# A linear-attention and GLU block on one core: VectorE work, transposes and a last tile moved between the steps

## The chip, the core and the metric

The kernel runs on one core of one Trainium2 chip. The metric is the device time of one execution in microseconds, the median of several runs. The profile beside it is that of one execution. Engines in it: PE is TensorE, PEld its weight loads, DVE VectorE, ACT ScalarE, POOL GpSimd, SP the engine that issues the transfers.

## The reference

One transformer block over 2048 tokens of width 512, all in float32. Six vectors of 512 (shift, scale and gate for each half) come from `silu(c) @ w_mod`.

```python
h = _layernorm(x) * (1 + ca) + sa
qkv = (h @ wqkv) ...                      # 32 heads of 16
pq, pk = phi(q), phi(k)                   # phi(t) = where(t > 0, t + 1, exp(t)) + 1e-6
kv = einsum("bhsd,bhse->bhde", pk, v);  z = einsum("bhsd->bhd", pk)
o = einsum(pq, kv) / (einsum(pq, z) + 1e-6)
x = x + ga * (o @ wo)
h = _layernorm(x) * (1 + cb) + sb
x = x + gb * (((h @ w_gate) * (h @ w_up)) @ w_down)     # F = 1376
```

## The kernel before

**Numbers and splits.** Every matrix that TensorE multiplies is held as a high part, rounded to fp32r on ScalarE, and a low part, the difference, taken on VectorE or GpSimd (`split`, lines 182 to 184). A product is then three matmuls: high by high, high by low, low by high.

**Tiling.** The 2048 tokens are four chunks (ch) of 512, each of four token tiles (j) of 128; token tile i is 4 ch + j. F is cut into ten tiles of 128 and one of 96. The three last ones, f0, f1 and f2 (`lone`, f2 has 96 rows), are worked plainly for chunks 0 and 1: `gate_up` makes the gate and the up product of one F tile (24 matmuls of 128x512, lines 683 to 702), multiplies them (line 699) and splits the result into kh and kl; `down` multiplies these with the down weights into four accumulator banks and its `take` adds them to x (`evac`, line 677). All else of the GLU goes through `block` (lines 855 to 903): for two chunks and one F tile at a time it forms seven products of half matrices instead of eight, in the order p1, p5, p6, p2, p7, p3, p4, six matmuls each, on four fixed PSUM banks a, b, c, d. ScalarE copies bank to bank (line 842), VectorE adds (lines 892 and 896) and multiplies (line 865). `down_group` (lines 905 to 919) is the down product of a group of F tiles; at the very end `by_tile` makes it finish one token tile after the other, and `evac` adds and sends each to the output (lines 677 and 679).

**The attention's second half.** For each token tile, `den_c` divides phi(q) by the denominator (line 509), `turn` transposes it (`turn_a`, line 578) and splits it (`turn_h` on ScalarE, line 582; `turn_l` on VectorE, line 586), `y_seed` writes the old x into a bank (line 605), `y_a` adds twelve matmuls of y to it (line 614), and `y_b` copies the result to x (line 619) and takes its statistics (lines 225, 226). When the four tiles of a chunk are there, `rstd_of` takes the power on GpSimd (line 234), `nmr_of` the product of mean and rstd on VectorE (line 237), `xhat` normalises on ScalarE (line 243), and `ln2_turn` transposes (line 250) and modulates (lines 262, 272, 273); chunks 2 and 3 go to DRAM (`kept`) and come back as the left operands of `block` (`Left`, whose sums are line 755). `Right` holds the right operands: `sums` (line 805), `high` (lines 816 and 819, ScalarE) and `lows` (line 823, GpSimd).

**What sets the order.** The schedule is manual: each engine issues its instructions in the order in which the code records them, and waits for the semaphores that its operands and buffers need. So the program text from line 1003 on is the order of each engine's queue. PSUM has two pools of four banks, `acc` and `bank`; a tile that is asked for while all are in use waits for the oldest to be read. `ffn` (lines 957 to 997) is a generator that yields after each product of `block`, and `fill(n)` (line 999) lets n of them be recorded; so the sequence of `fill` calls between lines 1128 and 1150 sets how the products of the first blocks stand among the last y products. Inside a block, `p6` scales the down weights (line 970), `p7` records the split of the next block's right operand, `p3` the split of the down weights (high on ScalarE, low on GpSimd), `p4` the sums of the block after it.

Of the kernel before, what the change touches and what calls it, by code (L numbers as in the profile page):

```python
# [11 lines left out]
ALU = mybir.AluOpType  # L12
AX = mybir.AxisListType

P = 128
# [7 lines left out]
def tile_adaln_block(  # L23
# [12 lines left out]
    nc = tc.nc  # L36
    ctx.enter_context(tc.manual_schedule())
    _, S, D = x.shape
    F = w_gate.shape[1]
    KD = D // P  # L40
    NJ = 4
# [10 lines left out]
    ov = out[0].rearrange("(c p j) d -> c j p d", p=P, j=NJ)  # L52
# [26 lines left out]
    def acc_bank():  # L79
        return T(ps_acc, "acc")  # L80
# [311 lines left out]
    rows, cols = {}, {}  # L392
# [27 lines left out]
    ahead = {2: proj(2, wk)}  # L420
    for i in range(NT):
        ch, j = divmod(i, NJ)
# [81 lines left out]
    def den_c(*tiles):  # L504

        for i in tiles:
            ch, j = divmod(i, NJ)
            p3 = phq[i].rearrange("p (h i) -> p h i", i=DH)
            nc.vector.scalar_tensor_tensor(p3, p3, EPS_PHI, dens[ch][:, j].unsqueeze(2).to_broadcast([P, NH, DH]),
                                           op0=ALU.add, op1=ALU.mult)  # L510
# [20 lines left out]
    ps = proj(6, wq)  # L531
    fs, tt = [], []
    for k in range(KD):
        f = B("n")
# [9 lines left out]
    for g in range(KD):  # L544
        a, b = g * P, (g + 1) * P
# [4 lines left out]
    ps = proj(8, wq)  # L550
# [9 lines left out]
    ps = proj(9, wq)  # L560
# [27 lines left out]
    def turn(i):  # L588
        turn_a(i)
        turn_h(i)  # L590
        turn_l(i)
# [7 lines left out]
    def y_seed(i, of=acc_bank):  # L599

        yps[i] = of()
        if of is bank:

            nc.tensor.matmul(yps[i], wp[0][0][:, :P], wp[0][0], start=True, stop=True)
        nc.scalar.activation(yps[i], xts[i // NJ][i % NJ], AF.Copy)
# [10 lines left out]
    def y_b(i):  # L616
        ch, j = divmod(i, NJ)
        ps = yps.pop(i)
        nc.scalar.activation(xts[ch][j], ps, AF.Copy)
        norm2[ch].stats(j, of=ps)  # L620

    def y_step(i, *more, late=(), q=None, turn=True, seed=acc_bank):

        if q is not None:
            ps = proj(q, wq)
        if turn and i + 1 < NT and i + 1 not in pqs:
            turn_a(i + 1)
        y_a(i)
        if i + 1 in tps:
            turn_h(i + 1)  # L630
            turn_l(i + 1)
        if i - 1 in yps:
            y_b(i - 1)
        if q is not None:
            q_a(q, ps)
        if seed and i + 1 < NT:
            y_seed(i + 1, seed)
        for do in more:
            do()
        for do in late:  # L640
            do()

    norm2 = {}
# [3 lines left out]
    wf = {}  # L647
# [23 lines left out]
    def prepare(f):  # L671
        return lambda: (scale_down(f), split_ffn(f))

    def evac(ch, dn, js=range(NJ), last=False):
        for j in js:
            xt = xts[ch][j]
            nc.vector.tensor_tensor(xt, dn[j], xt, op=ALU.add)  # L677
            if last:
                nc.sync.dma_start(ov[ch, j], xt)

    hs = {}

    def gate_up(ch, f):

        n = fts[f][1]
        gps, ups = bank(), bank()
        for w, ps in ((wf[f][0], gps), (wf[f][1], ups)):
            for k in range(KD):
                hh, hl = norm2[ch].t[k]
                nc.tensor.matmul(ps[:n], w[0][:, k], hh, start=k == 0, stop=False)  # L690
                nc.tensor.matmul(ps[:n], w[0][:, k], hl, start=False, stop=False)  # L691
                nc.tensor.matmul(ps[:n], w[1][:, k], hh, start=False, stop=k == KD - 1)  # L692

        def rest():
            g = B("phi")
            h = B("kh", dt=F32R)
            l = B("kl", dt=F32R)
            nc.scalar.activation(g[:n], gps[:n], AF.Copy)
            nc.vector.tensor_tensor(g[:n], ups[:n], g[:n], op=ALU.mult)
            split(g[:n], h[:n], l[:n])  # L700
            hs[ch, f] = h, l
        return rest

    def down(ch, js=range(NJ), ahead={}, parts=(lone,)):

        dn = {j: acc_bank() for j in js}
        for step, (part, j) in enumerate((part, j) for part in parts for j in js):
            for do in ahead.get(step, ()):
                do()
            a, b = j * P, (j + 1) * P  # L710
            for f in part:
                n = fts[f][1]
                (hh, hl), (dh, dl) = hs[ch, f], wf[f][2]
                nc.tensor.matmul(dn[j], hh[:n, a:b], dh[:n], start=f == lone[0], stop=False)
                nc.tensor.matmul(dn[j], hh[:n, a:b], dl[:n], start=False, stop=False)
                nc.tensor.matmul(dn[j], hl[:n, a:b], dh[:n], start=False, stop=f == lone[-1])
        return lambda: evac(ch, dn, js)
# [184 lines left out]
        also("p4")  # L902
        yield

    def down_group(ch, side, js, outs, ds, last, by_tile=False):

        dn = {j: acc_bank() for j in js}
        hs = [out[side] for out in outs]
        order = [(i, j) for i in range(len(hs)) for j in js]
        if by_tile:  # L910
            order.sort(key=lambda ij: ij[1])
        for i, j in order:
            (hh, hl), (dh, dl) = hs[i], ds[i]
            a, b = j * P, (j + 1) * P
            n = hh.shape[0]
            nc.tensor.matmul(dn[j], hh[:, a:b], dh[:n], start=i == 0, stop=False)  # L916
            nc.tensor.matmul(dn[j], hh[:, a:b], dl[:n], start=False, stop=False)  # L917
            nc.tensor.matmul(dn[j], hl[:, a:b], dh[:n], start=False, stop=i == len(hs) - 1)  # L918
        return lambda: evac(ch, dn, js, last)

    groups = [((0, 1), g) for g in ((0, 1), (2, 3), (4, 5), (6, 7))]
    groups += [((2, 3), g) for g in ((10, 0, 1), (2, 3, 4), (5, 6, 7), (8, 9))]
# [7 lines left out]
    def right_sums(n, on=None):  # L930
        if n < len(steps):
            rights[n].sums(on)
# [20 lines left out]
    side = {}  # L953
    free = [False]
    parts = []

    def ffn():

        first_side, second_side = side, {}
        m = 0  # L960
        for g, (cs, fs) in enumerate(groups):
            last = g + 1 == len(groups) or groups[g + 1][0] != cs
            outs, ds = [], []
            A = first_side if cs == (0, 1) else second_side
            for f in fs:
                out = []
                draw = draws.pop(m)

                def scale(d=draw):
                    nc.vector.tensor_tensor(d, d, gb[:d.shape[0]], op=ALU.mult)  # L970

                at = {"p6": [scale],
                      "p7": [lambda: draw_load(m + 1), lambda: right_load(m + 2), lambda: right_split(m + 1)],
                      "p3": [lambda: ds.append(split_raw(draw, low=nc.gpsimd))],
                      "p4": [lambda: right_sums(m + 2)]}
                for point in ("p1", "p5", "p2", "p3", "p4")[2 if m == 2 else 0:]:
                    at.setdefault(point, []).append(lambda: some(some_at.get(m, 0)))
                if m + 1 < len(steps) and steps[m + 1][0] != cs:
                    at["p1"].append(lambda: fetch(stash, second_side, "a11", "s1"))
                    at["p7"].insert(0, lambda: fetch(stash, second_side, "s2", "a12", "s3"))  # L980
                elif m and steps[m - 1][0] != cs:
                    at["p1"].append(lambda: fetch(stash, second_side, "s4", "a22"))
                outs.append(out)
                yield from block(A, rights[m], out, at)
                m += 1
                if free[0] and parts:
                    takes = [down_group(*p) for p in parts.pop(0)]
                    yield
                    for take in takes:
                        take()  # L990
            cut_at = {2: ([[0, 1, 2, 3], []], [[], [0, 1, 2, 3]]),
                      3: ([[0, 1, 2], []], [[3], [0, 1]], [[], [2, 3]])}[len((groups + groups[-1:])[g + 1][1])]
            parts.extend([(ch, i, js, outs, ds, last) for i, (ch, js) in enumerate(zip(cs, jss)) if js] for jss in cut_at)
        flush()
        while parts:
            for p in parts.pop(0):
                down_group(*p, by_tile=not parts)()

    def fill(n):
        for _ in range(n):  # L1000
            next(work, None)

    f0, f1, f2 = lone
    turn_a(0)
    ps = proj(11, wq)
# [56 lines left out]
    y_b(7)  # L1062
    norm2[1].rstd_of()
    den_b(2)
    take = down(0)
    ln2_nx(1)
    den_c(8, 9, 10)
    turn(8)
    y_seed(8, bank)
    take()  # L1070
    ln2_turn(1, 0, 1)
    y_step(8)
# [23 lines left out]
    g()  # L1096
    norm2[2].xhat(2, 3)
    turn_a(12)
    take = down(1, (0, 1))
    turn_h(12)  # L1100
    turn_l(12)
    den_c(13)
# [8 lines left out]
    take = down(1, (2, 3))  # L1111
# [15 lines left out]
    work = ffn()  # L1127
    y_step(14, seed=None)
    fill(1)
    y_seed(15, y_bank)  # L1130
    first[0].split("s3", "s4")
    fill(1)
    first[1].split("s3", "s4")
    right_sums(1, nc.vector)
    fill(2)
    y_step(15)
    y_b(15)
    norm2[3].rstd_of()
    fill(2)
    norm2[3].nmr_of()  # L1140
    fill(2)
    norm2[3].xhat(0)
# [40 lines left out]
```

## Time and profile before

| | us |
|---|---|
| median of 3 runs | 572.92 (571.94 to 573.11) |
| span of the profiled execution | 570.9 |
| TensorE busy | 560.6 (98%) |
| VectorE busy | 373.8 (65%) |
| ScalarE busy | 279.7 (49%) |
| GpSimd busy | 185.6 (33%) |

Of the profiled execution the page gives the span, from its first to its last instruction; the runs are other executions and their times are measured from outside. The granted TensorE clock is full in every slice of the page. A row of a timeline has the start in us from the begin of the span, the duration in us, the engine, the line of the code, the operation, what it writes and reads by the program's names, the shapes and types, and how many like it stand merged in the row; in brackets stands the time that the engine was idle before it and what ended that. A row of a group has, behind the count, the busy time in us, the mean of one in ns, and the idle time before. A row of one line's view has minimum, median and maximum in ns. A row of windows has the stretch, its length, and the busy time and number of instructions of PE, PEld, DVE, ACT and POOL, then granted clock, share of the DMA engines and GB/s. Matmul records overlap: each lasts longer than the distance to the next one's start.

### The profile page before, as it was taken

What the parts mean: (1) busy time and instruction counts of PE and PEld (TensorE: products, weight loads), DVE (VectorE), ACT (ScalarE), POOL (GpSimd) and SP (SyncE); (2) the same over time, 40 slices, a digit from 0 to 9 for tenths busy, and PEclk for the clock granted to TensorE, in tenths of its full rate; (3) what the DMA queues carried; (4) which work ended last, traced back from release to release, by engine and by line L of the source; (5) the groups of instructions that cost most, each with busy time, mean ns of one, the idle gap of its engine ahead of it and who ended that gap; (6) DMA issues with size and microseconds to landing.
All of it is one profiled execution on the core that took longest, in us unless ns stands there. A gap on an engine that the chain in (4) does not pass through costs nothing.

```text
span 570.9 us, 7343 instructions
## 1 busy us (share of the span) xinstructions
PE 560.6 (98%) x2569; PEld 457.3 (80%) x2569; DVE 373.8 (65%) x613; ACT 279.7 (49%) x500; POOL 185.6 (33%) x191
## 2 busy tenths in 40 slices
PE   7999999999999999999989999999999999999997
PEld 6778888888888778878878888887888888888885
DVE  6876868868768876768776777755554434344444
ACT  3785857546456535445865545533333333334110
POOL 2000000000011300000389666665667446556200
PEclk9999999999999999999999999999999999999999
DMA  8900223302301000804208462699436122100004
GB/s 279 378 6 2 73 75 102 121 0 57 96 0 52 24 1 37 258 0 136 68 2 276 147 209 93 218 337 335 126 110 174 29 56 55 57 18 2 0 1 147
DMA packets 50165, 59.34 MB, mean 104 GB/s; under 512 B 6416, under 2 KB 26896, under 8 KB 50128
## 3 DMA queue, kind: packets, MB, share of 16 engines
q1 hardware_dynamic: 50128, 58.87, 32.0%
q8 instruction: 20, 0.33, 0.2%
q14 instruction: 17, 0.14, 0.1%
HBM read 43.12 MB, written 15.73 MB: 103 GB/s over the span
## 4 chain that ended last, share of the span: by engine, by line
PE 88%; DVE 4%; ACT 2%; DMA 2%; POOL 2%; issue 1%; SPq 0%; POOLq 0%; DVEq 0%; ACTq 0%
PE bank L837 28%; PE acc L614 7%; PE acc L916 6%; PE acc L917 6%; PE acc L918 6%; PE bank L198 5%; PE bank L196 5%; PE bank L197 5%; PE acc L329 3%; PE acc L328 3%; PE acc L327 3%; PE bank L691 2%; PE bank L692 2%; PE bank L690 2%; PE bank L250 1%; PE bank L578 1%
## 5 line engine op out<-in xcount | busy, mean ns | idle before, releaser
L837 PE MATMUL bank<-h,w 128*128 128x512 f32 (+1 forms) x798 | 185.3, 390 | 1.6 <-DVE u L892 1.6
L837 PEld LDWEIGHTS bank<-h,w 128*128 128x128 f32 (+1 forms) x798 | 148.2, 186 | 34.9 <-DVE u L892 2.5
L842 ACT ACTIVATE bank<-bank 128x512 f32<-128x512 f32 (+1 forms) x38 | 22.2, 583 | 144.7 <-PE bank L837 144.7
L677 DVE TENSOR_TENSOR x<-acc,x 128x512 f32<-128x512 f32 x72 | 48.9, 690 | 49.2 <-PE acc L918 48.5
L823 POOL TENSOR_TENSOR w<-raw,w 128x256 fp32r<-128x256 f32 (+3 forms) x38 | 42.2, 1111 | 97.0 <-ACT w L816 76.7
L184 POOL TENSOR_TENSOR w<-raw,w 128x512 fp32r<-128x512 f32 (+1 forms) x25 | 35.5, 1422 | 115.9 <-DVE mv L226 87.5
L916 PE MATMUL acc<-w,kh 128*128 128x512 f32 (+1 forms) x152 | 59.2, 390 | 0.0
L917 PE MATMUL acc<-w,kh 128*128 128x512 f32 (+1 forms) x152 | 59.2, 390 | 0.0
L918 PE MATMUL acc<-w,kl 128*128 128x512 f32 (+1 forms) x152 | 59.1, 389 | 0.0
L234 POOL TENSOR_TENSOR rstd<-ve,half 128x4 f32<-128x4 f32 (+1 forms) x9 | 9.4, 1045 | 138.2 <-DVE ve L233 136.6
L184 DVE TENSOR_TENSOR kl<-u,kh 128x512 fp32r<-128x512 f32 (+1 forms) x38 | 27.4, 761 | 34.5 <-ACT kh L183 32.6
L823 POOL TENSOR_TENSOR w<-t,w 128x512 fp32r<-128x512 f32 (+1 forms) x38 | 48.0, 1286 | 0.0
L196 PE MATMUL bank<-w,h 128*128 128x512 f32 x112 | 44.9, 401 | 0.0
L198 PE MATMUL bank<-w,h 128*128 128x512 f32 x112 | 43.9, 392 | 0.0
L197 PE MATMUL bank<-w,h 128*128 128x512 f32 x112 | 43.6, 389 | 0.0
L614 PE MATMUL acc<-w,xh 128*128 128x512 f32 x120 | 38.1, 398 | 0.0
L916 PEld LDWEIGHTS acc<-w,kh 128*128 128x128 f32 (+1 forms) x152 | 28.5, 188 | 6.0
L918 PEld LDWEIGHTS acc<-w,kl 128*128 128x128 f32 (+1 forms) x152 | 28.5, 188 | 6.0
L917 PEld LDWEIGHTS acc<-w,kh 128*128 128x128 f32 (+1 forms) x152 | 28.5, 188 | 6.0
L243 ACT ACTIVATE n<-x,nmr,rstd 128x512 f32<-128x512 f32 x32 | 24.1, 805 | 17.2 <-DVE nmr L237 17.2
L892 DVE TENSOR_TENSOR u<-bank,u 128x512 f32<-128x512 f32 (+1 forms) x19 | 13.1, 691 | 28.8 <-PE bank L837 28.8
L183 ACT ACTIVATE w<-raw 128x512 fp32r<-128x512 f32 (+2 forms) x44 | 26.4, 618 | 3.2 <-DMA raw<-in_A_wqkv_dram 2.2
(177 smaller groups left out, 1098.1 us busy)
## 6 DMA issues: line engine op xcount, KB each, us to landing
raw<-in_w_mod_dram SPq DMA_DIRECT2D x24, 256.0 KB, 3.7
raw<-in_B_w_down_dram SPq DMA_DIRECT2D x20, 256.0 KB, 3.0
raw<-in_B_w_gate_dram SPq DMA_DIRECT2D x36, 128.0 KB, 3.5
raw<-in_B_w_up_dram SPq DMA_DIRECT2D x36, 128.0 KB, 3.6
x<-in_A_x_dram SPq DMA_DIRECT2D x16, 256.0 KB, 5.4
kept<-f SPq DMA_DIRECT2D x16, 256.0 KB, 2.1
f<-kept SPq DMA_DIRECT2D x16, 256.0 KB, 4.6
side_s<-h SPq DMA_DIRECT2D x16, 256.0 KB, 2.9
```

What stands on the lines that cost most here:

```text
L183: nc.scalar.activation(h, src, AF.Copy)
L184: (low or nc.vector).tensor_tensor(l, src, f32(h), op=ALU.subtract)
L196: nc.tensor.matmul(ps, ah, bh, start=i == 0, stop=False)
L197: nc.tensor.matmul(ps, ah, bl, start=False, stop=False)
L198: nc.tensor.matmul(ps, al, bh, start=False, stop=i == n - 1)
L614: nc.tensor.matmul(yps[i], x, y, start=False, stop=k == KD - 1 and x is al, skip_group_check=True)
L677: nc.vector.tensor_tensor(xt, dn[j], xt, op=ALU.add)
L823: sub = lambda out, x, y: (on or nc.gpsimd).tensor_tensor(out, x, f32(y), op=ALU.subtract)
L837: mm = lambda x, y, **kw: nc.tensor.matmul(ps, x[:, k], y, skip_group_check=True, **kw)
L916: nc.tensor.matmul(dn[j], hh[:, a:b], dh[:n], start=i == 0, stop=False)
L917: nc.tensor.matmul(dn[j], hh[:, a:b], dl[:n], start=False, stop=False)
L918: nc.tensor.matmul(dn[j], hl[:, a:b], dh[:n], start=False, stop=i == len(hs) - 1)
```

## The change

Five edits. `gate_up` works the gate and the up product side by side, block by block of the normalised input. In `down(0)`, the transposes and the split of token tile 8, its seed, and the divisions of tiles 9 and 10 are recorded ahead of the fourth token tile's matmuls. In `down(1, (0, 1))` the products with F tiles f0 and f1 of both token tiles stand ahead of those with f2. Around the last y products, tile 14's copy and statistics come ahead of tile 15's seed, the sums of the second right operand ahead of two splits of left operands, and tile 15's copy, its statistics, `rstd_of` and `nmr_of` after the two products p7 and p3. In the last `down_group`, the last token tile is done in two halves of 256 columns, each added and sent by itself.

```diff
-    def evac(ch, dn, js=range(NJ), last=False):
+    def evac(ch, dn, js=range(NJ), last=False, cols=((0, D),)):
         for j in js:
             xt = xts[ch][j]
-            nc.vector.tensor_tensor(xt, dn[j], xt, op=ALU.add)
-            if last:
-                nc.sync.dma_start(ov[ch, j], xt)
+            for a, b in cols:
+                nc.vector.tensor_tensor(xt[:, a:b], dn[j][:, a:b], xt[:, a:b], op=ALU.add)
+                if last:
+                    nc.sync.dma_start(ov[ch, j, :, a:b], xt[:, a:b])
...
-        for w, ps in ((wf[f][0], gps), (wf[f][1], ups)):
-            for k in range(KD):
-                hh, hl = norm2[ch].t[k]
+        for k in range(KD):
+            hh, hl = norm2[ch].t[k]
+            for w, ps in ((wf[f][0], gps), (wf[f][1], ups)):
                 nc.tensor.matmul(ps[:n], w[0][:, k], hh, start=k == 0, stop=False)
...
-    def down_group(ch, side, js, outs, ds, last, by_tile=False):
+    def down_group(ch, side, js, outs, ds, last, by_tile=False, end=False):
+
+        hs = [out[side] for out in outs]
+
+        def mm(ps, i, j, c, d):
+            (hh, hl), (dh, dl) = hs[i], ds[i]
+            a, b = j * P, (j + 1) * P
+            n = hh.shape[0]
+            nc.tensor.matmul(ps, hh[:, a:b], dh[:n, c:d], start=i == 0, stop=False)
+            nc.tensor.matmul(ps, hh[:, a:b], dl[:n, c:d], start=False, stop=False)
+            nc.tensor.matmul(ps, hl[:, a:b], dh[:n, c:d], start=False, stop=i == len(hs) - 1)
 
         dn = {j: acc_bank() for j in js}
-        hs = [out[side] for out in outs]
-        order = [(i, j) for i in range(len(hs)) for j in js]
+        tail = js[-1:] if end else []
+        order = [(i, j) for i in range(len(hs)) for j in js if j not in tail]
         if by_tile:
             order.sort(key=lambda ij: ij[1])
         for i, j in order:
...
-        return lambda: evac(ch, dn, js, last)
+            mm(dn[j], i, j, 0, D)
+
+        def take():
+            evac(ch, dn, [j for j in js if j not in tail], last)
+            for j in tail:
+                other = acc_bank()
+                for ps, c, d in ((dn[j], 0, D // 2), (other, D // 2, D)):
+                    for i in range(len(hs)):
+                        mm(ps[:, c:d], i, j, c, d)
+                    evac(ch, {j: ps}, [j], last, ((c, d),))
+        return take
...
         while parts:
-            for p in parts.pop(0):
-                down_group(*p, by_tile=not parts)()
+            group = parts.pop(0)
+            for p in group:
+                down_group(*p, by_tile=not parts, end=not parts and p is group[-1])()
...
-    take = down(0)
     ln2_nx(1)
-    den_c(8, 9, 10)
-    turn(8)
-    y_seed(8, bank)
+    den_c(8)
+    take = down(0, ahead={3: (lambda: turn(8), lambda: y_seed(8, bank), lambda: den_c(9, 10))})
     take()
...
-    take = down(1, (0, 1))
+    take = down(1, (0, 1), parts=((f0, f1), (f2,)))
...
     fill(1)
+    y_b(14)
     y_seed(15, y_bank)
+    right_sums(1, nc.vector)
     first[0].split("s3", "s4")
     fill(1)
     first[1].split("s3", "s4")
-    right_sums(1, nc.vector)
     fill(2)
     y_step(15)
+    fill(2)
     y_b(15)
     norm2[3].rstd_of()
-    fill(2)
     norm2[3].nmr_of()
     fill(2)
```

More of the change, by code (lines that the diff above doesn't have):

```diff
@@ L912, in down_group @@
         for i, j in order:
[L913 to L918, printed above, removed]
-        return lambda: evac(ch, dn, js, last)
+            mm(dn[j], i, j, 0, D)
[8 more added lines that the diff above has]
+        return take
     groups = [((0, 1), g) for g in ((0, 1), (2, 3), (4, 5), (6, 7))]
```

## The prediction, as it was put on record before the changed kernel ran

> **What bounds the kernel now.** I read the page's busy shares, the chain of work that ended last, and then the engines' timelines at the five places that the diff touches, from which the fences pick rows.
>
> ```profile
> PE 560.6 (98%) x2569; PEld 457.3 (80%) x2569; DVE 373.8 (65%) x613; ACT 279.7 (49%) x500; POOL 185.6 (33%) x191
> ...
> 283.32 2.88 PE L837 MATMUL bank<-h,w 128*128 128x512 f32 x12
> ```
>
> TensorE is the bound, 98% busy. A busy share hides short stops, because a matmul's record (0.39 us in the rows below) is longer than the step to the next one. So I read starts: twelve matmuls in 2.88 us are steps of (2.88 - 0.39) / 11 = 0.227 us, and a larger step is a stop. The change can win only such stops and the tail behind the last matmul.
>
> **Gate and up side by side.** Before, the first gate/up step uses each normalised block for three matmuls and then needs the next:
>
> ```profile
> 183.56 0.48 PE L690 MATMUL bank<-h,w 128*128 128x512 f32 x1
> 183.87 0.40 PE L691 MATMUL bank<-h,w 128*128 128x512 f32 x1
> 185.94 0.50 PE L691 MATMUL bank<-h,w 128*128 128x512 f32 x1 [0.23 <-DVE h L273]
> 190.34 0.60 PE L578 MATMUL bank<-ident,h 128*128 128x128 f32 x4
> 185.20 0.69 DVE L273 TENSOR_TENSOR h<-f,h 128x512 fp32r<-128x512 f32 x1
> 186.26 0.69 DVE L273 TENSOR_TENSOR h<-f,h 128x512 fp32r<-128x512 f32 x1
> 187.75 3.01 POOL L184 TENSOR_TENSOR w<-raw,w 128x512 fp32r<-128x512 f32 x2 [6.73 <-PE bank L692]
> 182.00:191.00 9.00, 8.64 (x42) 6.36 (x41) 8.86 (x15) 5.22 (x9) 3.01 (x2) 1.00 0.26 95
> ```
>
> The low parts of blocks 2 and 3 are ready at 185.89 and 186.95. With six matmuls to a block they are needed from 183.56 + 0.31 (the first step) + 11 x 0.227 = 186.4 and 187.7: nothing waits. The 24 matmuls end their issue at 183.56 + 0.31 + 23 x 0.227 = 189.1 in place of 190.34: **1.24** won. What is late next is the low half of the following up weights (GpSimd, 187.75 + 3.01 = 190.76): up now needs it as sixth matmul, near 190.67, instead of as fifteenth; with a restart that costs 0.2. VectorE is nearly full here (8.86 of 9.00 us, the third figure of the window), so later y steps could still wait for it; I follow that as a rival. Value 1.0, between 0 and 1.25. The other gate/up steps are not stopped; the gate bank is copied later but still 0.7 before up ends, about the length of the copy: nothing.
>
> **Transposes inside the down product.**
>
> ```profile
> 217.40 1.89 DVE L509 SCALAR_TENSOR_TENSOR h<-h,den 128x512 f32<-128x512 f32 x3
> 217.52 2.94 ACT L243 ACTIVATE n<-x,nmr,rstd 128x512 f32<-128x512 f32 x4 [2.55 <-DVE nmr L237]
> 220.29 0.39 PE L714 MATMUL acc<-w,kh 128*128 128x512 f32 x1
> 223.63 0.69 DVE L586 TENSOR_TENSOR xl<-bank,xh 128x512 fp32r<-128x512 f32 x1 [4.33 <-ACT xh L582]
> 223.03 1.04 PE L250 MATMUL bank<-ident,n 128*128 128x128 f32 x8
> 224.38 0.66 PE L578 MATMUL bank<-ident,h 128*128 128x128 f32 x4 [0.31 <-DVE xl L586]
> L250 PE MATMUL bank<-ident,n 128*128 128x128 f32 x96 | 12.4, 272 | 0.0
> ```
>
> Transposes of token tile 9 need the bank of tile 8, whose low part lands at 224.32. Moved to 220.29, ahead of the last token tile of the down product, tile 8's transposes end near 220.9; ScalarE is free from 220.46, so xl ends near 222.3, and the two divisions moved behind it (0.6 each) near 223.5. Tile 9's division is done at 222.9. Transposes step at (1.04 - 0.27) / 7 = 0.11, eight of them 0.87, so tile 9 starts at 223.03 + 0.87 = 223.9 instead of 224.38: **0.5** won (0.4 to 0.55). The four evacuations start near 223.4, no later than before.
>
> **Two parts in the second down product.**
>
> ```profile
> 254.54 0.48 PE L714 MATMUL acc<-w,kh 128*128 128x512 f32 x1
> 256.07 0.69 DVE L184 TENSOR_TENSOR kl<-phi,kh 96x512 fp32r<-96x512 f32 x1 [0.70 <-ACT kh L183]
> 259.24 1.04 PE L250 MATMUL bank<-ident,n 128*128 128x128 f32 x8
> ```
>
> The 96-row tile's product is ready at 256.76 and was wanted as seventh to ninth matmul, from 254.54 + 0.32 + 5 x 0.23 = 256.0. Behind twelve others it is wanted at 257.4. Eighteen at 0.23 end at 254.54 + 0.09 + 18 x 0.23 = 258.8 in place of 259.24: **0.45** won (0.3 to 0.5).
>
> **VectorE around the last y product.** Here the largest stop stands, and a new queue is built.
>
> ```profile
> 287.66 2.58 PE L837 MATMUL bank<-h,w 128*128 128x512 f32 x10 [1.45 <-DVE u L892]
> 286.91 0.69 DVE L892 TENSOR_TENSOR u<-bank,u 128x512 f32<-128x512 f32 x1
> 288.85 1.29 DVE L237 SCALAR_TENSOR_TENSOR nmr<-mv,rstd 128x4 f32<-128x4 f32 x1
> 290.06 0.68 DVE L865 TENSOR_TENSOR u<-bank,u 128x512 f32<-128x512 f32 x1
> 284.15 0.43 ACT L816 ACTIVATE w<-raw 128x256 fp32r<-128x256 f32 x1
> 287.15 1.01 POOL L234 TENSOR_TENSOR rstd<-ve,half 128x4 f32<-128x4 f32 x1 [9.83 <-DVE ve L233]
> 288.12 0.75 POOL L823 TENSOR_TENSOR w<-raw,w 128x256 fp32r<-128x256 f32 x1
> 294.27 1.19 POOL L805 TENSOR_TENSOR t<-raw 128x256 f32<-128x256 f32 x1
> 291.30 1.14 ACT L183 ACTIVATE kh<-u 128x512 fp32r<-128x512 f32 x2
> 293.52 0.60 ACT L842 ACTIVATE bank<-bank 128x512 f32<-128x512 f32 x1
> 298.04 0.63 ACT L819 ACTIVATE w<-t 128x512 fp32r<-128x512 f32 x1 [0.47 <-POOL t L805]
> 299.62 2.77 ACT L262 ACTIVATE f<-acc,col,col 128x512 f32<-128x512 f32 x4
> 309.03 1.66 PE L837 MATMUL bank<-h,w 128*128 128x512 f32 x6 [0.17 <-DVE u L892]
> L237 DVE SCALAR_TENSOR_TENSOR nmr<-mv,rstd x9: 153/161/1293, 9.2 to 288.8; 128x4 f32<-128x4 f32 x7, 128x2 f32<-128x2 f32 x2
> ```
>
> Before, L892 stands behind both statistics on VectorE. Twelve matmuls from 283.32 would allow the next at 286.1; it starts at 287.66, so 1.6 are lost. After, tile 14's statistics go into the idle time before tile 15's seed, tile 15's go behind the block's additions, L892 comes near 285.2, and this stop goes. But the power for rstd (L234) is now issued after the next block's weight splits: on GpSimd it stands behind five operations, which took 288.12 to 294.27, 6.15 us. ScalarE reaches their first input 0.95 earlier (two y copies of 0.5 leave its queue), so GpSimd could start at 283.6; I add 0.35, half of a VectorE subtraction that now ends about there, and the power runs near 290.1 to 291.2. nmr waits for it; behind nmr on VectorE waits the product c*p5 (L865), behind that on ScalarE the kh copy of it, one xhat and the block's three bank copies.
>
> What nmr costs: 0.16 by the median, 1.29 in the row at 288.85, where GpSimd had begun a 128x512 step at about the same moment. After, GpSimd's next operation (a 128x256 sum, 0.73 to 1.19) starts in the instant the power ends, so I take 0.9: c*p5 ends at 292.1 + 0.6 = 292.7, against 290.74 before. (The Trainium skill, "SBUF — State Buffer", section "Who interferes with whom", says that a VectorE instruction with two SBUF inputs and a GpSimd one that reads SBUF exclude each other, the second waiting until the first has finished. The row at 288.85 agrees.)
>
> From there I copy the distances of before. The second kh began at 291.30 + 0.52 and the copy of bank c ended at 294.12, 2.3 later; now that kh begins at 292.75 and c is ready at 295.05. TensorE restarts on bank a when a*u2 has read it (two 0.7 additions and products behind 286.3, so 287.8) and comes to c's reader 24 matmuls later, at 293.25: a new stop of 1.8. The modulated copies (L262) started 7.8 after that kh, 0.47 of it idle for GpSimd's sums, which now are early: 292.75 + 7.3 = 300.0 against 299.62. Their tiles go to DRAM and back ahead of the L892 that holds TensorE at 309.03, so this place ends near 309.4. **Instead of 1.6 won, 0.4 lost.** Ends: 1.3 won (TensorE alone is the limit), 2.2 lost (four of GpSimd's steps held by 0.45 each, the difference of its two 128x256 rows, 0.75 and 1.19).
>
> **Last token tile in halves.**
>
> ```profile
> 566.44 0.39 PE L918 MATMUL acc<-w,kl 128*128 128x512 f32 x1
> 566.87 0.69 DVE L677 TENSOR_TENSOR x<-acc,x 128x512 f32<-128x512 f32 x1 [0.67 <-PE acc L918]
> 271.13 0.41 DVE L805 TENSOR_TENSOR t<-raw 128x256 f32<-128x256 f32 x1
> out_dram<-x SPq DMA_DIRECT2D x8, 256.0 KB, 2.4
> L918 PEld LDWEIGHTS acc<-w,kl 128*128 128x128 f32 (+1 forms) x152 | 28.5, 188 | 6.0
> ```
>
> Six matmuls of 512 columns become twelve of 256. No row shows that width: 128-column transposes step at 0.11, each with its own weight load, so 0.12 each is nearest: 12 x 0.12 - 6 x 0.227 = 0.1 lost; if the 188 ns weight load does not overlap, 0.9 lost. VectorE's last addition goes from 0.69 to about 0.42 (the 256-column row): 0.27 won. The last transfer halves: between nothing and half of 2.4; I take 0.25, near nothing. One more transfer is issued, beside the product. **0.4 won** (0.6 lost to 1.4 won). The Trainium skill, "DMA: Bandwidth & Descriptors", section "Anatomy of one DMA — SWDGE (gpsimd) path", speaks against more: about 2 us are fixed and only bytes / 436e3 us scale; an estimate by that, for a path that this queue is not, is 0.3. No row shows it.
>
> **Sum.** 1.0 + 0.5 + 0.45 - 0.4 + 0.4 = 1.95. The profiled span is 570.9, so 568.95 after. The median of the runs, 572.92, is 2.0 above that span; I leave this distance: **570.97**.
>
> **Rivals.**
> - The y edit pays: nmr isn't held and GpSimd finishes early, so TensorE alone limits at 1.3 won instead of 0.4 lost: 569.3. For it: GpSimd was idle 9.83 before the power. Against: five splits now fill that.
> - The first edit is taken back: VectorE, full from 182 to 191, makes the next y steps wait, and the 1.0 goes: 572.0. Against: the waits of the y products that I followed come within about 0.1 us of TensorE but not past it.
> - Slower: GpSimd and VectorE alternate through the splits. With the five splits, the power and the first sum held by 0.45 each, c*p5 ends 7 x 0.45 = 3.15 later, at 295.85, and the place loses 3.55 in place of 0.4: 574.1. It outweighs the 2.35 of the other edits once c*p5 ends after 292.3 (292.7 less the 0.4) + 2.35 = 294.65, that is from the fifth held step. For it: the held rows of before. Against: in that stretch VectorE has only the draw's scaling and nmr with two SBUF inputs.
> - That the edits do not take effect: each changes the order on its engine directly, so I give it nothing.
>
> **How the numbers follow.** About 0.2%, 1.15 us, can be told from no change: faster means below 571.77, slower above 574.07. Forecast 0.56, own range 570.0 to 571.7. Y edit pays 0.18. First edit taken back 0.16, of which a quarter falls below 571.77. Slower 0.10, a third of it within 0.2%. Faster 0.56 + 0.18 + 0.04 = 0.78; same 0.12 + 0.03 = 0.15; slower 0.07. The range holds the first three cases with part of the bounds of the y edit and the tail, 569.0 to 572.6.
>
> **What would show it.** Right: no step over 0.25 between 183.9 and 189 on TensorE; tile 9's transposes directly behind the eight of L250; no stop in the second down product; the stop at 287.66 gone, one of 1 to 2 us some 7 us later at the reader of bank c, with the power behind the five splits on GpSimd. Wrong: TensorE reaching the modulated tiles over 0.5 us earlier relative to the last y product, or half-width matmuls stepping at 0.19.

## The result, and the profile after

The changed kernel takes **570.45 us** (median of 6 runs, 569.81 to 571.12) where the kernel before takes 572.03 (6 runs beside it, 571.85 to 573.11): ratio 0.9968, 95% interval 0.9957 to 0.9979, that is 1.58 us less (1.2 to 2.5). The profiled execution took 570.02, with a span of 568.3 against 570.9.

The head of the page of the changed kernel:

```profile
span 568.3 us, 7356 instructions
PE 560.3 (99%) x2575; PEld 458.8 (81%) x2575; DVE 373.1 (66%) x614; ACT 279.8 (49%) x500; POOL 186.2 (33%) x191
```

TensorE does the same work, plus six records for the halved tile, in a span that is 2.6 shorter, so what went is idle time. Where it went can be read by matching the two executions: the same matmul is looked up in both traces, and its start in the one is subtracted from its start in the other. The table gives how this difference changes from one time of the kernel before to the next; a minus is time won. "Ahead" is the difference at 181 us, before the first edit, and belongs to no edit. "Tail" is the rest up to the difference of the spans. (E1 to E11 are the experiments below. All differences between 404 and 564 us are zero.)

| kernel | ahead | gate/up 181-195 | first down 195-247 | second down 247-274 | y 274-300 | left sums 300-311 | 311-373 | 373-404 | tail | span |
|---|---|---|---|---|---|---|---|---|---|---|
| changed | -0.67 | -0.99 | -0.61 | -0.37 | 0.33 | -0.44 | 0.57 | 0.00 | -0.41 | -2.60 |
| E1 old y order | -0.82 | -1.00 | -0.61 | -0.37 | -0.01 | 0.73 | -0.06 | 0.00 | -0.42 | -2.56 |
| E2 y edit alone | -0.46 | -0.01 | -0.01 | 0.05 | 0.35 | -0.37 | 0.56 | 0.39 | -0.01 | 0.51 |
| E3 gate/up alone | -0.10 | -1.00 | -0.02 | 0.09 | -0.04 | 0.05 | 0.56 | 0.00 | 0.00 | -0.47 |
| E4 downs alone | 0.16 | 0.01 | -0.59 | -0.46 | -0.05 | 0.07 | 0.55 | 0.00 | 0.00 | -0.32 |
| E5 whole tail | -0.58 | -1.00 | -0.61 | -0.37 | 0.35 | 0.18 | 0.55 | 0.00 | 0.00 | -1.47 |
| E6 late nmr | -0.99 | -0.95 | -0.61 | -0.37 | -1.19 | 0.53 | -0.05 | 0.00 | -0.41 | -4.05 |
| E7 off p2 | -0.62 | -0.96 | -0.61 | -0.37 | 0.35 | -0.47 | 1.25 | 0.00 | -0.41 | -1.83 |
| E8 old y, off p2 | -1.01 | -0.95 | -0.61 | -0.37 | -0.01 | -0.47 | 1.25 | 0.00 | -0.42 | -2.58 |
| E9 one point | -0.54 | -1.01 | -0.61 | -0.37 | 0.35 | -0.43 | 0.00 | 0.57 | -0.41 | -2.44 |
| E10 late nmr, late sum | -0.56 | -0.97 | -0.61 | -0.37 | -1.20 | -0.47 | -0.06 | 0.85 | -0.41 | -3.80 |
| E11 late nmr, both | -0.50 | -0.97 | -0.61 | -0.37 | -1.19 | -0.47 | -0.01 | 0.00 | -0.41 | -4.53 |

The edits act at their places with the same size in every kernel that has them, to 0.1. What differs between kernels is "left sums" and the two columns behind it, where none of the five edits stands (E7 to E11 move other steps there). Behind the first edit the changed kernel's spans differ by 2.60 - 0.67 = 1.93.

**The three stops that went.** The changed kernel's matmuls at the first gate/up step, at the transposes in the first down product, and at the second down product (PE timeline):

```profile
182.91 0.48 PE L691 MATMUL bank<-h,w 128*128 128x512 f32 x1
183.23 0.40 PE L692 MATMUL bank<-h,w 128*128 128x512 f32 x1
...
188.27 0.39 PE L693 MATMUL bank<-h,w 128*128 128x512 f32 x1
188.50 0.60 PE L578 MATMUL bank<-ident,h 128*128 128x128 f32 x4
...
221.37 1.04 PE L250 MATMUL bank<-ident,n 128*128 128x128 f32 x8
222.25 0.60 PE L578 MATMUL bank<-ident,h 128*128 128x128 f32 x4
...
252.25 0.48 PE L715 MATMUL acc<-w,kh 128*128 128x512 f32 x1
256.49 1.04 PE L250 MATMUL bank<-ident,n 128*128 128x128 f32 x8
```

The 24 matmuls take 188.50 - 182.91 = 5.59 where the kernel before took 190.34 - 183.56 = 6.78: 1.19 won. Tile 9's transposes come 0.88 behind the start of L250's eight (1.35 before), and the second down product takes 4.24 (4.70 before). One row further on stands the new wait of the first edit, for the low half of the next up weights (all engines of the changed kernel):

```profile
187.11 3.00 POOL L184 TENSOR_TENSOR w<-raw,w 128x512 fp32r<-128x512 f32 x2 [6.75 <-ACT w L183]
190.16 0.19 PEld L693 LDWEIGHTS bank<-h,w 128*128 128x128 f32 x1 [0.33 <-POOL w L184]
```

It takes back the other 0.2 of the 1.19.

**The y products.** Around the last y product (all engines of the changed kernel; a row ends with what ended the idle time):

```profile
285.23 5.72 PE L838 MATMUL bank<-h,w 128*128 128x512 f32 x24 [0.31 <-DVE u L866]
286.21 1.29 POOL L184 TENSOR_TENSOR w<-raw,w 128x512 fp32r<-128x512 f32 x1
287.46 1.01 POOL L234 TENSOR_TENSOR rstd<-ve,half 128x4 f32<-128x4 f32 x1
288.50 0.69 DVE L237 SCALAR_TENSOR_TENSOR nmr<-mv,rstd 128x4 f32<-128x4 f32 x1 [2.23 <-POOL rstd L234]
289.12 0.68 DVE L866 TENSOR_TENSOR u<-bank,u 128x512 f32<-128x512 f32 x1
289.83 0.63 ACT L183 ACTIVATE kh<-u 128x512 fp32r<-128x512 f32 x1 [1.76 <-DVE u L866]
290.37 0.80 ACT L243 ACTIVATE n<-x,nmr,rstd 128x512 f32<-128x512 f32 x1
291.55 0.58 ACT L843 ACTIVATE bank<-bank 128x512 f32<-128x512 f32 x1
292.19 3.02 PE L838 MATMUL bank<-h,w 128*128 128x512 f32 x12 [1.24 <-ACT bank L843]
```

Read upward from the last row: TensorE waits for the copy of bank c, that copy stands on ScalarE behind an xhat (L243, which needs nmr itself) and a kh whose product c*p5 (L866 at 289.12) comes late, c*p5 stands on VectorE behind nmr, and nmr waits 2.23 for the power, which GpSimd begins in the moment when the last split before it ends. The 24 matmuls unstopped would have led to 285.23 + 24 x 0.227 = 290.68; the stop is 1.5.

**The tail.** TensorE and VectorE of the changed kernel at the end:

```profile
563.12 0.28 PE L914 MATMUL acc<-w,kh 128*128 128x256 f32 x1
563.23 0.28 PE L915 MATMUL acc<-w,kh 128*128 128x256 f32 x1
...
564.43 0.28 PE L916 MATMUL acc<-w,kl 128*128 128x256 f32 x1
564.75 0.42 DVE L678 TENSOR_TENSOR x<-acc,x 128x256 f32<-128x256 f32 x1 [0.29 <-PE acc L916]
```

Eleven steps take 564.43 - 563.12 = 1.31, 0.12 each: a 256-column step is half of a 512-column one and no more. The last matmul's end stands 568.3 - 564.71 = 3.59 ahead of the end of the span, before 570.9 - 566.83 = 4.07.

### The profile page after: what moved, and what is told of

Read it like the earlier page. It is cut to its first block, busy times and chain, and to the rows that moved or that the text cites. A ratio compares the mean times of both kernels' runs of the same rounds, so it can differ in the third digit from the quotient of the medians.

```text
span 568.3 us, 7356 instructions
## 1 busy us (share of the span) xinstructions
PE 560.3 (99%) x2575; PEld 458.8 (81%) x2575; DVE 373.1 (66%) x614; ACT 279.8 (49%) x500; POOL 186.2 (33%) x191
## 4 chain that ended last, share of the span: by engine, by line
PE 89%; DMA 3%; issue 2%; POOL 1%; DVE 1%; ACT 1%; SPq 1%; POOLq 0%; ACTq 0%
PE bank L838 28%; PE acc L914 6%; PE acc L915 6%; PE acc L916 6%; PE acc L614 6%; PE bank L198 5%; PE bank L196 5%; PE bank L197 5%; PE acc L329 3%; PE acc L327 3%; PE acc L328 3%; PE bank L693 2%; PE bank L691 2%; PE bank L692 2%; PE bank L250 2%
## 5 line engine op out<-in xcount | busy, mean ns | idle before, releaser
L678 DVE TENSOR_TENSOR x<-acc,x 128x512 f32<-128x512 f32 (+1 forms) x73 | 49.1, 684 | 49.0 <-PE acc L916 48.2
L914 PE MATMUL acc<-w,kh 128*128 128x512 f32 (+2 forms) x154 | 59.6, 387 | 0.0
L915 PE MATMUL acc<-w,kh 128*128 128x512 f32 (+2 forms) x154 | 59.6, 387 | 0.0
L916 PE MATMUL acc<-w,kl 128*128 128x512 f32 (+2 forms) x154 | 59.5, 386 | 0.0
L243 ACT ACTIVATE n<-x,nmr,rstd 128x512 f32<-128x512 f32 x32 | 24.1, 804 | 17.2 <-DVE nmr L237 15.9
L262 ACT ACTIVATE f<-bank,col,col 128x512 f32<-128x512 f32 x28 | 20.7, 775 | 14.5 <-PE bank L250 12.4
```

Of the source, the lines that this page charges most:

```text
L243: nc.scalar.activation(self.n[j], self.tiles[j], AF.Identity, scale=self.rstd[:, j:j + 1], bias=self.nmr[:, j:j + 1])
L678: nc.vector.tensor_tensor(xt[:, a:b], dn[j][:, a:b], xt[:, a:b], op=ALU.add)
L914: nc.tensor.matmul(ps, hh[:, a:b], dh[:n, c:d], start=i == 0, stop=False)
L915: nc.tensor.matmul(ps, hh[:, a:b], dl[:n, c:d], start=False, stop=False)
L916: nc.tensor.matmul(ps, hl[:, a:b], dh[:n, c:d], start=False, stop=i == len(hs) - 1)
```

## The experiments

Diffs of E1 and E5 to E11 are against the changed kernel, those of E2 to E4 against the kernel before. The ratio is that to the kernel before run beside it, with its 95% interval.

**E1, the old order around the last y products.**

```diff
     fill(1)
-    y_b(14)
     y_seed(15, y_bank)
-    right_sums(1, nc.vector)
     first[0].split("s3", "s4")
     fill(1)
     first[1].split("s3", "s4")
+    right_sums(1, nc.vector)
     fill(2)
     y_step(15)
-    fill(2)
     y_b(15)
     norm2[3].rstd_of()
+    fill(2)
     norm2[3].nmr_of()
```

> The changed kernel with the block around the last two y products in the old order; the other four edits stay. Queue theory (the y edit trades one stop for another, because the power of rstd stands behind GpSimd's splits): 1.6 to 2.3 us below the kernel before, so no slower than the changed kernel by more than 0.3; on TensorE the long stop of about 1.6 us behind the last y product is back, the one at the reader of bank c is gone, and the stop ahead of the twelve matmuls that follow the modulated tiles (0.56 us in before) is back. Rival (the y edit pays 1.3 and the gate/up edit is taken back): 0.3 to 0.9 us below the kernel before, 0.7 to 1.3 slower than the changed kernel.

Measured: 569.83, ratio 0.9957 (0.9944 to 0.9969), 2.3 less than before. The y edit pays nothing; its rival, 0.3 to 0.9 less than before, is out. The old stop behind the y product is back and the one at bank c is gone (0.33 in the changed kernel's y column, -0.01 here). The stop ahead of the matmuls near 307 us is back and longer, by 0.73, than before. This run's rows there:

```profile
305.08 1.21 DVE L756 TENSOR_TENSOR s<-f,f 128x512 f32<-128x512 f32 x1 [1.32 <-POOL t L806]
306.22 0.68 DVE L893 TENSOR_TENSOR u<-bank,u 128x512 f32<-128x512 f32 x1
306.95 1.43 PE L838 MATMUL bank<-h,w 128*128 128x512 f32 x5 [0.90 <-DVE u L893]
```

GpSimd had begun a split at 305.01 (0.74), just ahead of the sum. So the sum of the left side takes 1.21 us here; it took 0.70 in the kernel before, where GpSimd began its split 0.10 behind it:

```profile
307.68 0.70 DVE L755 TENSOR_TENSOR s<-f,f 128x512 f32<-128x512 f32 x1 [1.14 <-DMA f<-kept]
```

The addition that TensorE needs is queued behind the sum.

**E2, E3 and E4, edits alone.** E2 is the kernel before with the hunk of E1 the other way round; E3 has only the loops of `gate_up` exchanged; E4 only the two lines of the down products:

```diff
-    take = down(0)
     ln2_nx(1)
-    den_c(8, 9, 10)
-    turn(8)
-    y_seed(8, bank)
+    den_c(8)
+    take = down(0, ahead={3: (lambda: turn(8), lambda: y_seed(8, bank), lambda: den_c(9, 10))})
...
-    take = down(1, (0, 1))
+    take = down(1, (0, 1), parts=((f0, f1), (f2,)))
```

> The kernel before with only the y edit. Queue theory: within 0.5 us of the kernel before; a stop of 0.3 to 0.5 us behind the last y product, one of 1.2 to 1.8 us some 7 us later at the reader of bank c, with the power behind the five splits on GpSimd. Rival (it pays): 1.3 us faster, and no stop over 0.5 us at the reader of bank c. Third theory (GpSimd and VectorE alternate through the splits): 1 us or more slower.

> The kernel before with only gate and up side by side. Theory: 1.0 us faster (0.7 to 1.25), all of it won within the first gate/up step, and TensorE 1.0 earlier from there to the end. Rival (VectorE is full there and the next y steps take the gain back): within 0.3 us of the kernel before, TensorE first 1 us earlier and then level by the end of the second y product.

> The kernel before with only the two edits of the down products (transposes inside the first, two parts in the second). Theory: 0.95 us faster (0.7 to 1.0), 0.5 at the transposes of tile 9 and 0.45 in the second down product. Rival (what is won there is waited for at the next fixed wait, the modulated tiles' way through DRAM and back): at most 0.3 us faster, with a longer stop ahead of the matmuls that follow those tiles.

Measured: E2 572.59, ratio 1.0009 (0.9999 to 1.0018); E3 572.06, 0.9994 (0.9985 to 1.0003); E4 572.05, 0.9996 (0.9987 to 1.0005). E2 is where the queue theory put it, and its trace has the stop at the reader of bank c too (1.25 idle ahead of that matmul, for the copy of the bank). E3 and E4 miss: 0.1 less instead of 1.0 and 0.95. Their traces show that the gains are there (-1.00; -0.59 and -0.46), and also that neither rival is right, since TensorE keeps them, to 0.1, past the y products and past 311 us. Both then lose 0.55 near 366 us, in a stop that the kernel before and E1 do not have, and the changed kernel and E2 have as well. The rows of the kernel before at this place:

```profile
366.57 0.63 ACT L183 ACTIVATE h<-f 128x512 fp32r<-128x512 f32 x1
...
367.31 0.69 DVE L184 TENSOR_TENSOR h<-f,h 128x512 fp32r<-128x512 f32 x1 [0.29 <-ACT h L183]
367.59 1.02 POOL L823 TENSOR_TENSOR w<-raw,w 128x256 fp32r<-128x256 f32 x1 [5.50 <-ACT w L816]
367.94 0.69 DVE L892 TENSOR_TENSOR u<-bank,u 128x512 f32<-128x512 f32 x1
```

And of E3:

```profile
365.55 0.63 ACT L183 ACTIVATE h<-f 128x512 fp32r<-128x512 f32 x1
...
366.56 0.74 POOL L823 TENSOR_TENSOR w<-raw,w 128x256 fp32r<-128x256 f32 x1 [5.51 <-ACT w L816]
366.64 1.22 DVE L184 TENSOR_TENSOR h<-f,h 128x512 fp32r<-128x512 f32 x1 [0.64 <-ACT w L816]
367.78 0.68 DVE L892 TENSOR_TENSOR u<-bank,u 128x512 f32<-128x512 f32 x1
368.51 1.20 PE L837 MATMUL bank<-h,w 128*128 128x512 f32 x4 [0.26 <-DVE u L892]
```

The same three instructions, those of VectorE and GpSimd in the other order. Where VectorE's subtraction starts first it takes 0.69 and GpSimd's split stretches from 0.74 to 1.02; where GpSimd is first, the subtraction takes 1.22, ending 0.56 behind GpSimd's end, and L892 behind it comes too late for TensorE. The Trainium skill, "SBUF — State Buffer", section "Who interferes with whom", says that the order of issue decides who blocks; the two fences agree, with 0.3 lost by the one and 0.5 by the other. The changed kernel has the same, with GpSimd's split begun at 364.83:

```profile
364.90 1.22 DVE L184 TENSOR_TENSOR h<-f,h 128x512 fp32r<-128x512 f32 x1 [0.64 <-ACT w L817]
```

**E5, the last tile whole.**

```diff
-                down_group(*p, by_tile=not parts, end=not parts and p is group[-1])()
+                down_group(*p, by_tile=not parts)()
```

> The changed kernel with the last token tile whole again; the other four edits stay. Theory: 0.2 to 0.5 us slower than the changed kernel (TensorE's twelve half-width matmuls cost 0.1 to 0.2, the shorter last addition and the halved last transfer give 0.5 to 0.6 back), that is 1.0 to 1.5 below the kernel before. Rival (a transfer's time is mostly fixed and TensorE's loss eats the rest): within 0.1 of the changed kernel.

Measured: 571.16, ratio 0.9979 (0.997 to 0.9988), 0.7 above the changed kernel's 570.45. The tail is 0.41 of it by the trace, as the theory says. The rest stands elsewhere: near 305 us, where the code is the same in both, the changed kernel won 0.44 and this run lost 0.18. Its rows:

```profile
305.08 0.73 POOL L824 TENSOR_TENSOR w<-raw,w 128x256 fp32r<-128x256 f32 x1
305.28 1.08 DVE L756 TENSOR_TENSOR s<-f,f 128x512 f32<-128x512 f32 x1 [0.76 <-DMA f<-kept]
306.28 0.68 DVE L893 TENSOR_TENSOR u<-bank,u 128x512 f32<-128x512 f32 x1
307.01 1.65 PE L838 MATMUL bank<-h,w 128*128 128x512 f32 x6 [0.35 <-DVE u L893]
```

And of the changed kernel:

```profile
304.80 0.77 DVE L756 TENSOR_TENSOR s<-f,f 128x512 f32<-128x512 f32 x1 [0.38 <-DMA f<-kept]
304.98 1.19 POOL L824 TENSOR_TENSOR w<-raw,w 128x256 fp32r<-128x256 f32 x1
305.49 0.68 DVE L893 TENSOR_TENSOR u<-bank,u 128x512 f32<-128x512 f32 x1
```

Measured against TensorE, the tiles came back 0.4 later from DRAM, so GpSimd's split began ahead of the sum and held it: one instruction order at this place, 0.62 us apart in two executions.

**E6, nmr later.**

```diff
     norm2[3].rstd_of()
+    fill(2)
     norm2[3].nmr_of()
     fill(2)
     norm2[3].xhat(0)
-    fill(2)
     norm2[3].xhat(1)
```

> The changed kernel with nmr of the last chunk issued behind two more steps of the block, and its first two xhats together behind two more. Theory (c*p5 and the copy of bank c are late only because nmr, queued ahead of them on VectorE, waits for the power behind GpSimd's splits): the 1.4 us stop at the reader of bank c goes, and TensorE comes to the matmuls behind the modulated tiles about 1.4 earlier; of that 0.3 to 1.4 is kept, since there it may wait for those tiles' way through DRAM, so 0.3 to 1.4 us faster than the changed kernel. Rival (the copies of bank c wait for something else, the kh copies or GpSimd itself): the stop stays within 0.3 of its length, and the time within 0.3 us.

Measured: **568.56**, ratio 0.9934 (0.992 to 0.9948), 1.9 below the changed kernel, more than the 0.3 to 1.4 expected. The rows that answer to those of the changed kernel:

```profile
284.95 8.45 PE L838 MATMUL bank<-h,w 128*128 128x512 f32 x36 [0.31 <-DVE u L866]
285.92 0.68 DVE L866 TENSOR_TENSOR u<-bank,u 128x512 f32<-128x512 f32 x1
287.19 1.00 POOL L234 TENSOR_TENSOR rstd<-ve,half 128x4 f32<-128x4 f32 x1
289.36 0.58 ACT L843 ACTIVATE bank<-bank 128x512 f32<-128x512 f32 x1 [0.56 <-PE bank L838]
289.59 0.70 DVE L237 SCALAR_TENSOR_TENSOR nmr<-mv,rstd 128x4 f32<-128x4 f32 x1
```

The power is as late as it was (287.19, behind the same splits), but c*p5 no longer stands behind nmr: it runs at 285.92, the copy of bank c at 289.36, and 36 matmuls follow each other without a stop. So the splits alone cost nothing here; the queues behind nmr did. This edit moves the first xhat behind the copies as well, so it does not part what nmr held on VectorE from what that xhat held on ScalarE. The y column goes from 0.33 to -1.19. The wait for the left sums took 0.53 back, as expected, but the stop near 366 us did not occur.

**E7 and E8, no draws at p2.** The left side of the second chunk pair is worked off one step at a time at given points of the blocks. In both, nothing is drawn at p2, right ahead of VectorE's addition to bank c; E8 has E1's hunk too.

```diff
-                for point in ("p1", "p5", "p2", "p3", "p4")[2 if m == 2 else 0:]:
+                for point in ("p1", "p5", "p3", "p4")[2 if m == 2 else 0:]:
...
-    stash, some_at = {}, {m: 1 for m in range(2, 7)}
+    stash, some_at = {}, {2: 1, 3: 1, 4: 1, 5: 2, 6: 2}
```

> The changed kernel with the sums and splits of the second chunk pair's left side no longer drawn at the point of a block that comes right before VectorE's addition to bank c (p2), but at the four other points, two at a time in the last two of these blocks. Collision theory (the 0.57 us stop near 366 us, which the kernel before doesn't have, comes from a VectorE subtraction of that left side that GpSimd's split holds right before the addition): that stop goes and the kernel is 0.4 to 0.6 us faster than the changed one. Rival (the collision only moves to another point, or two operations at once make a new one): within 0.2 us of the changed kernel, or slower.

> The changed kernel with the block around the last two y products in the old order, and the left side's sums and splits not drawn at p2. In the kernel with the old y order alone TensorE stops 1.29 us ahead of the matmuls near 307 us, where VectorE's addition stands behind the first such sum, which waits for the modulated tiles' way through DRAM and is then held by GpSimd. Theory (the sum is what holds the addition): that stop goes, and the kernel is 0.9 to 1.3 us faster than with the old y order alone, near 568.7. Rival (other waits are as late there: the addition's own bank, or GpSimd's splits): at most 0.3 us faster than it, near 569.6.

Measured: E7 570.67, ratio 0.9969 (0.9957 to 0.998), no better than the changed kernel; E8 570.75, 0.9968 (0.9956 to 0.9981), 0.9 worse than E1. In E8's trace the stop near 307 us is gone, as the theory said (-0.47 where E1 has 0.73). But both lose 1.25 before 373 us. The rows of E7:

```profile
363.12 0.62 ACT L183 ACTIVATE h<-f 128x512 fp32r<-128x512 f32 x1
363.64 0.62 ACT L183 ACTIVATE h<-s 128x512 fp32r<-128x512 f32 x1
364.16 0.59 ACT L843 ACTIVATE bank<-bank 128x512 f32<-128x512 f32 x1
364.80 1.90 PE L838 MATMUL bank<-h,w 128*128 128x512 f32 x7 [0.76 <-ACT bank L843]
```

Two draws at a point put two high parts on ScalarE ahead of its copies of banks, and TensorE waits for those: a new stop in place of the old, as the rival had it.

**E9, one point left out.**

```diff
-                for point in ("p1", "p5", "p2", "p3", "p4")[2 if m == 2 else 0:]:
+                for point in (("p1", "p5", "p3", "p4") if m == 6 else ("p1", "p5", "p2", "p3", "p4")[2 if m == 2 else 0:]):
```

> The changed kernel with one draw of the second chunk pair's left side taken away: in the block that has the 0.57 us stop near 366 us (the seventh of eight) nothing is drawn at p2, so its later subtractions come one point later; no two are drawn at once. Collision theory: that stop goes and nothing takes its place, 0.4 to 0.6 us faster than the changed kernel, near 569.9. Rival (the stop moves to the next point, as where two were drawn at once it had grown to 0.92): within 0.2 us of the changed kernel.

Measured: 570.72, ratio 0.9977 (0.9964 to 0.9989; 12 runs from 569.91 to 573.19), not faster. The stop near 366 us is gone (0.00 in the column):

```profile
364.47 0.74 POOL L824 TENSOR_TENSOR w<-raw,w 128x256 fp32r<-128x256 f32 x1 [4.99 <-ACT w L817]
365.34 0.69 DVE L893 TENSOR_TENSOR u<-bank,u 128x512 f32<-128x512 f32 x1 [0.92 <-PE bank L838]
```

GpSimd still begins first, and the addition, with no subtraction ahead of it, is on time. So the held subtraction was that stop. A stop of the same size stands near 397 us instead. There TensorE's weight loads wait for left operands on their way back from DRAM, which they do not in the changed kernel:

```profile
397.37 0.16 PEld L838 LDWEIGHTS bank<-h,w 128*96 128x96 f32 x1 [0.42 <-DMA h<-side_a]
397.98 0.24 PEld L838 LDWEIGHTS bank<-h,w 128*96 128x96 f32 x2 [0.45 <-DMA h<-side_a]
```

So the collision theory is half right: the stop goes, but something takes its place. What made those operands later is not shown.

**E10 and E11, the late nmr with the first sum moved.** Both have E6's hunk. In E10 the draws begin at p3 of the third block; E11 draws two at p3 there and none at p2 of the seventh.

```diff
-                for point in ("p1", "p5", "p2", "p3", "p4")[2 if m == 2 else 0:]:
+                for point in ("p1", "p5", "p2", "p3", "p4")[3 if m == 2 else 0:]:
```

and, in E11,

```diff
-                for point in ("p1", "p5", "p2", "p3", "p4")[2 if m == 2 else 0:]:
+                for point in {2: ("p3", "p3", "p4"), 6: ("p1", "p5", "p3", "p4")}.get(m, ("p1", "p5", "p2", "p3", "p4")):
```

> The kernel with the late nmr, and the draws of the left side begin one point later (p3 of the third block in place of p2), so that the first sum, which waits for the modulated tiles' way through DRAM, stands behind VectorE's two additions in place of ahead of them. Theory (in the run with the late nmr TensorE stops 0.83 us near 304 us for that sum alone): the stop goes, 0.6 to 0.9 us faster than with the late nmr alone, near 567.8, unless a subtraction one point later is caught by GpSimd's split near 364 us, which would take 0.57 back. Rival (the tiles' way through DRAM holds something else there as well, the later steps): at most 0.3 us faster than with the late nmr alone.

> The kernel with the late nmr, nothing drawn at p2 in the third and in the seventh block, and two draws at p3 of the third. Theory: both the stop near 304 us (0.83 with the late nmr alone) and the possible one near 364 us are gone, near 567.7 us, and no step of TensorE above 0.5 us between 290 and 560 us. Rival (two sums at p3 hold the products behind them, or the draws collide at other points): a new stop of 0.3 us or more there, and no faster than the late nmr with the later sum.

Measured: E10 568.85, ratio 0.9935 (0.9921 to 0.9949); E11 **568.50**, 0.993 (0.9918 to 0.9942). Expected were 567.8 and 567.7. In both traces the wait for the left sums is gone (-0.47 where E6 has 0.53). E10 then lost 0.85 near 397 us, where it waited for left operands on their way back from DRAM as E9 did (weight loads up to 0.56, a matmul 0.3). The wait of the matmul:

```profile
PE bank L838 <- DMA h<-side_a: 0.3, 1, 0.3
```

E11's trace has no stop of TensorE from 290 us to the end and is the shortest, 566.4. Its median is still within 0.1 of E6's, whose trace has a stop of 0.8. The theory is right in the profiled execution; by the medians the rival (no faster than the late nmr alone) cannot be refuted. E6 and E11 are the fastest kernels of the study, about 3.8 us below the kernel before.

## Why the prediction was right, step by step

The forecast was 1.95 us won; the runs show 1.58 (1.2 to 2.5), and the profiled executions 1.93 behind the start of the first edit. As a time the forecast, 570.97, lies 0.5 above the 570.45 measured although less was won than forecast, because the kernel before, run beside it, took 572.03 and not the 572.92 that the forecast started from.

- **Gate and up: 1.0 forecast, 0.99 measured**, with both parts of the working: 1.19 won in the step (1.24 forecast) and 0.2 lost to GpSimd's low half. The rival that VectorE takes it back in the y steps is refuted: in E3 TensorE keeps all but 0.1 of it to 311 us.
- **Transposes: 0.5 forecast, 0.61 measured** (0.47 of it at the transposes, 1.35 - 0.88). **Two parts: 0.45 forecast, 0.46** in the second down product (E4), of which 0.1 is lost again before 274 us in the changed kernel.
- **The y edit: 0.4 lost forecast, 0.33 lost measured** up to the modulated tiles. The stop at bank c was forecast at 1.8 and is 1.5, mostly since nmr cost 0.7 instead of the 0.9 taken. E6 shows that the named cause, the queues behind the late power, is the cause. The step that failed is the last one, "this place ends near 309.4": the wait behind the modulated tiles' way through DRAM, which the sum carried over from before, did not come in the changed kernel's trace, and 0.44 was won there, while E5, with the same code at that place, lost 0.18. It was counted as a distance, and it is a meeting of a transfer, a VectorE sum and GpSimd.
- **The tail: 0.4 forecast, 0.41 measured.** TensorE lost 0.07 (0.1), the last addition is 0.27 shorter as forecast, and 0.21 (0.25) is left for the transfer and the end.
- **Not in the forecast: 0.57 lost near 366 us**, some seventy us behind the y edit. The slower rival priced this mechanism (a step held by 0.45) but placed it in GpSimd's splits among the y products. There the first split took 1.47 in the changed kernel (0.75 in the row at 288.12 of the kernel before), the last was 0.44 shorter than before, and the five took 6.43 in place of 6.15 together. That the sum came out right rests on this loss and the 0.44 won at 305 us nearly cancelling each other, and that is luck.

What stays open: why VectorE's subtraction near 366 us starts 0.46 behind the end of the high part on ScalarE that it needs in E3 (365.55 + 0.63 = 366.18, to 366.64) and 0.11 behind it in the kernel before (366.57 + 0.63 = 367.20, to 367.31). It is the same in the other traces that have this order of instructions: 0.45 to 0.47 in the five with the stop, 0.10 or 0.11 in the kernel before, E1 and E6. This decides which engine is first. Of the executions without a profile it can't be seen which stops they have, so it is argued, not shown, that such stops make E3 and E4 gain 0.1 instead of 1.0, and make E11 no faster than E6. Nor does one trace stand for all runs of its kernel: behind 181 us the trace of E6 is 3.06 shorter than that of the kernel before where its median is 3.8 lower, and that of E1 1.74 where its median is 2.3 lower.

## What to carry to other kernels

An instruction that waits for a slow engine is to be recorded behind what the bounding engine needs next: the late power was harmless once nmr no longer stood ahead of a bank's product, nor the first xhat ahead of its copy (E6, 1.9 us), while the edit that had moved them together won nothing. A gain found at one place is only shown there; where VectorE and GpSimd both work from SBUF, which of them is first further on can give half a microsecond back, so edits of this size are judged by matching matmuls between traces as well as by the median. Moving such work to another point only helps where that point has room (E7 and E8 had none).

## What the runs showed of the hardware that was not expected

The same code at the same place differs by up to half a microsecond between executions: the sum L756 took 0.77 in the changed kernel and 1.08 in E5, and the subtraction near 366 us 0.69 in the kernel before and 1.22 in E3. And the halved matmuls step at 0.12 although each has a weight load of 0.19 by the profile, so the records of neighbouring loads overlap.
